# Two-layer H3/MLP training step on one core: where layer 2's normalised rows are kept, and the order of the k-gradient tail

## The chip, the cores and the metric

The kernel runs on one core of a Trainium2 chip. The metric is device time in microseconds for one launch. Before the change three runs gave 770.30, 773.59 and 775.28 us; the median is 773.59. A separate, profiled execution gave the trace that all readings of the kernel before come from.

## The reference

The kernel computes a forward pass and all gradients of it (outputs: the result and the gradients of q, k, v, shift_k, ssm_k, ssm_D, w1, w2). Sequence length S = 2048, width D = 448, hidden width F = 1792, bfloat16.

```
def A(q, k, v, shift_k, ssm_k, ssm_D):       # H3-like long convolution
    k_shift = sum over t of 4: k delayed by t rows * shift_k[:, 3 - t]
    kv = k_shift * v
    y  = irfft(rfft(kv, 2S) * rfft(ssm_k, 2S))[:S] + kv * ssm_D
    return q * y
def B(x, w1, w2):
    return silu(x @ w1) @ w2

x = A_q
for layer in (1, 2):
    x = x + A(layernorm(x), k, v, shift_k, ssm_k, ssm_D)
    x = x + B(layernorm(x), w1, w2)
return x, and vjp(grad_out)
```

The convolution term depends on k, v and the parameters alone, so both layers share it, and its gradient is taken once, from the sum of what both layers give.

## The kernel before

Everything is laid out with 128 partitions; a [2048, 448] matrix stands in on-chip memory as 128 x 16 x 448 (16 row groups, NT = 16). The program has three parts.

`_ssm_prefix` computes the convolution output once by a two-stage Fourier transform in matmuls. `Main.run` walks four chunks of 512 rows through forward and backward of both layers: `H` (x @ w1), `O` (@ w2), `G` (gradient @ w2 transposed, the tile `w2T`), `N` (@ w1 transposed). It leaves the activations and their gradients in device memory as `a_d` and `g_d`, and the normalised rows in `N_d`. `_ssm_suffix` takes the gradient of the convolution: a forward transform (`_fft_stage1`, L206, 16 rounds), transposes (L1095), `spectrum` (L1112), `inverse` (14 chunks of each of two kinds, L226 and L227, a chunk of the kind `cnd` and one of the other by turns), then the gradient with respect to kv (`ps_gkv`, L1169, 8 rounds), that of ssm_k (`ps_gK`, L1189, 8 rounds) with a one-column copy into `gKD` for ssm_D (L1193), that of shift_k (`ps_sk`, L1207, four rounds `r0` of 64, 64, 64 and 32 small matmuls, reduced on VectorE at L1212 to L1215 into `gskb`) and that of k (16 rounds `g` on VectorE, L1223 to L1226, with a store into output 2 after each odd round, L1228). Rounds `g` of 13 and more read three rows that a transfer moves from the next partition (L1177).

The weight gradients of w1 and w2 are done by `Jobs` as filler between the pieces of the third chunk and of the suffix. A job step is four matmuls of 128x448 (L906, or L941 in the opening). There are 224 steps: 24 of an opening, then groups of 8 (two passes of 16 matmuls) or, for the pairs (5, 6) and (12, 13), of 16. Each pass needs one `dstat` tile (512 KB, `load`, L900), loaded on SyncE's queue; the loads are kept in order by `issue_after(self.last_ld.ins)`. The moving operands are whole matrices: `go` (grad_out) and `X` for w2's gradient, `n3m` (layer 2's normalised rows, from `N_d[3]`) and `n1m` (layer 1's) for w1's, and `go2` (grad_out once more) for the rest of w2's. 34 steps run before the suffix; `jobs.run(n)` calls place the others, and `jobs.run(1000)` at the end runs what is left. `n3m` is first read at step 57, `n1m` at 61, `go2` at 169.

Four large places in memory are shared by tag. Before the change WT holds `w2T`, then `Zw` (three of the seven transposed blocks), then `ksf`; WY holds `Ysb` (the prefix's output, then its gradient, read by stage 1), then `n3m`, then `go2`; WB holds `go`, then `n1m`. A tile that follows another waits for the other's last reader. `load_n3` is called after stage 1, when `Ysb` has been read.

The order of TensorE's instructions is that of the program text (`manual_schedule`). For the other engines and the queues a scheduler orders the instructions when the program is built; each engine and queue then runs its list in order. The stores of the suffix are issued by GpSimd (POOL), and so are the loads of spectra and of k, v.

The tile `junk` of the shift gradient and the tile `s_` of the k gradient share one tag, `gka`, with one buffer, and the text puts the reduction of the shift gradient ahead of the 16 rounds.

Of the kernel before, what the change touches and what calls it, by code (L numbers as in the profile page):

```python
# [10 lines left out]
FP32 = mybir.dt.float32  # L11
# [6 lines left out]
P = 128  # L18
# [3 lines left out]
J = 16  # L22
# [816 lines left out]
class Jobs:  # L839
# [78 lines left out]
    def group(self, fts, keys, movs, fin, tags=None):  # L918
        ps = {}
        tags = tags or [None] * len(fts)  # L920
        for i, ft in enumerate(fts):
            st = self.load(keys[0], ft)
            ps[ft] = self.bank(tags[i])
            yield from self.mms(ps[ft], st, movs[0](), 0, NT, True, False)
        if fts == (12, 13):
            self.go2()
        for ft in fts:
            st = self.load(keys[1], ft)
            yield from self.mms(ps[ft], st, movs[1](), 0, NT, False, True)
            fin(ft, ps[ft])  # L930
# [34 lines left out]
    def go2(self):  # L965
        k = self.k
        if not hasattr(self, "go2t"):
            self.go2t = k.wk.tile([P, NT, D], BF16, name="go2", tag="WY")
            k.nc.sync.dma_start(out=self.go2t[:], in_=_pm(k.grad_out[0]))
        return self.go2t  # L970

# [6 lines left out]

    def load_n3(self):
        k = self.k  # L980
        self.n3 = k.wk.tile([P, NT, D], BF16, name="n3m", tag="WY")
        k.nc.sync.dma_start(out=self.n3[:], in_=_pm(k.N_d[3][:]))

    def out(self):
        return self.k.dp2.tile([P, D], BF16, name="dout", tag="dout", bufs=2)
# [64 lines left out]
def _ssm_suffix(k):  # L1050
# [9 lines left out]
    with ExitStack() as es:  # L1060
# [7 lines left out]
        for n2 in range(16):  # L1068
            k.M1sb = k.m1h[n2 // 8]
            _fft_stage1(k, n2, gY[:, n2, :], A1, psum, n2 % 8)  # L1070
            jobs.run(1)
        jobs.load_n3()
        _load_minv(k, nc.gpsimd)
        with ExitStack() as e1:
            p1 = e1.enter_context(tc.tile_pool(name="sspec2", bufs=1, reuse_waits="tile"))
            Zw = k.wk.tile([P, 3, 16, P], BF16, name="Zw", tag="WT")
            Z = [p1.tile([P, 16, P], BF16, name=f"Zg{g}") if g > 2 else Zw[:, g] for g in range(7)]
            Zf = [(z if isinstance(z, bass.AP) else z[:]).rearrange("p a b -> p (a b)") for z in Z]
            kk1 = p1.tile([P, 2, 2048], BF16, name="kk_d", tag="kk1")
            ap = APart(k, e1.enter_context(tc.tile_pool(name="qp", bufs=1, reuse_waits="tile")))  # L1080
            A1f = A1[:].rearrange("p a c n s -> p a (c n s)")

            def spec_load(cp):
                lo, hi = cp * 2048, (cp + 1) * 2048
                kk = (kk0 if cp == 0 else kk1 if cp == 1 else sp.tile([P, 2, 2048], BF16, name="kk_c", tag="kk0") if cp % 2 == 0
                      else p1.tile([P, 2, 2048], BF16, name="kk_d", tag="kk1"))
                nc.gpsimd.dma_start(out=kk[:, 0, :], in_=k.SPEC_d["K"][:, lo:hi])
                nc.gpsimd.dma_start(out=kk[:, 1, :], in_=k.SPEC_d["KV"][:, lo:hi])
                return kk

            kks = [spec_load(0)]
            for g in range(7):
                pt = psum.tile([P, 16, P], BF16, name="ps_tr", **mm)
                for i in range(16):
                    nc.tensor.transpose(pt[:, i, :], A1f[:, 16 * g + i, :], k.ident[:])  # L1095
                if g % 2:
                    nc.scalar.copy(Zf[g], pt[:].rearrange("p a b -> p (a b)"))
                else:
                    i = nc.vector.tensor_copy(Zf[g], pt[:].rearrange("p a b -> p (a b)"))
                jobs.run(1)  # L1100
                if g == 2:
                    ap.run(1, i)
            kks.append(spec_load(1))

            def spectrum(cp):
                xsw = p1.tile([P, 2048], BF16, name="xsw_c", tag="xsw", bufs=2)
                kk = kks[cp]
                for u in range(2):
                    ps = psum.tile([P, 1024], FP32, name="ps_s2", **mm)
                    for hh in range(2):  # L1110
                        c0 = u * 1024 + hh * 512
                        nc.tensor.matmul(ps[:, hh * 512:(hh + 1) * 512], lhsT=k.Gsb[:, G_FWD, :], rhs=Zf[cp][:, c0:c0 + 512], start=True, stop=True)  # L1112
                    nc.scalar.copy(Zf[cp][:, u * 1024:(u + 1) * 1024], ps[:])
                    jobs.run(1)
                _swap_halves(k, xsw, Zf[cp])
                return kk[:, 0, :], kk[:, 1, :], xsw

            def inverse(cp, t):
                for u in range(2):
                    ci = 2 * cp + u  # L1120
                    o = slice(u * 1024, (u + 1) * 1024)
                    for spec_t, B1, cnd in ((t[1], B1k, True), (t[0], B1v_, False)):
                        pa = p1.tile([P, 1024], BF16, name="pa", tag="pab", bufs=5)
                        pb = p1.tile([P, 1024], BF16, name="pb", tag="pab", bufs=5)
                        nc.vector.tensor_tensor(out=pa[:], in0=Zf[cp][:, o], in1=spec_t[:, o], op=ALU.mult)
                        last = nc.vector.tensor_tensor(out=pb[:], in0=t[2][:, o], in1=spec_t[:, o], op=ALU.mult)
                        bal.add("dve", 2.2)
                        _fft_inv_stage2_chunk(k, pa, pb, True, B1, ci, psum, cnd=cnd)
                        jobs.run(3)
                return last  # L1130

            prev = spectrum(0)
            for cp in range(NCI // 2):
                cur = spectrum(cp + 1) if cp + 1 < NCI // 2 else None
                ap.run(1, inverse(cp, prev))
                if cp + 2 < NCI // 2:
                    kks.append(spec_load(cp + 2))
                prev = cur

        p2 = es.enter_context(tc.tile_pool(name="sp2", bufs=1, reuse_waits="tile"))  # L1140
        ksf = k.wk.tile([P, J, D], BF16, name="ksf", tag="WT")
        gks = p2.tile([P, 19, D], BF16, name="gks")
        kx = p2.tile([P, 19, D], BF16, name="kx_s")
        nc.gpsimd.memset(kx[0:1, 0:3, :], 0.0)
# [36 lines left out]
        for dc in range(ND):  # L1181
            gK = p2.tile([DC, S], BF16, name="gK", tag="gK", bufs=3)
            gKv = gK[:].rearrange("p (n1 n2) -> p n1 n2", n2=16)
            for g in range(2):
                py = psum.tile([P, 8, P], FP32, name="ps_gK", **mm)
                for i in range(8):
                    n2 = 8 * g + i
                    for c in range(2):
                        nc.tensor.matmul(py[:DC, i, :], lhsT=B1k[:, 16 * c + n2, dc * DC:(dc + 1) * DC], rhs=k.Minvsb[:, n2, c, :], start=(c == 0), stop=(c == 1))  # L1189
                _copy(nc, nc.scalar, gKv[:, :, 8 * g:8 * g + 8], py[:DC].rearrange("p i n -> p n i"))  # L1190
                jobs.run(2)
            nc.gpsimd.dma_start(out=out5v[:, dc, :], in_=gK[:])
            nc.vector.tensor_copy(gKD[:, dc:dc + 1], gK[:, 0:1])  # L1193
        with nc.allow_non_contiguous_dma(reason="tiny g_D store"):
            nc.gpsimd.dma_start(out=k.outs[6].rearrange("(c p) -> p c", p=DC), in_=gKD[:])

# [5 lines left out]
        for r0 in range(4):  # L1202
            bands = 4 if r0 < 3 else 2
            for sl_ in range(16):
                for b in range(bands):
                    ch = slice(P * r0 + 32 * b, P * r0 + 32 * b + 32)
                    nc.tensor.matmul(pd[32 * b:32 * b + 32, 0, P * r0:P * r0 + P], lhsT=gks[:, sl_, ch], rhs=kx[:, sl_:sl_ + 4, ch], start=(sl_ == 0), stop=(sl_ == 15))  # L1207
        junk = p2.tile([P, 4, 4, 32], FP32, name="skjunk", tag="gka")
        gsk = p2.tile([P, 4, 4], FP32, name="gsk")
        gskb = p2.tile([P, 4, 4], BF16, name="gskb")  # L1210
        for n, lo, hi in ((P, 0, 3), (64, 3, 4)):
            nc.vector.tensor_tensor(out=junk[:n, lo:hi], in0=pd[:n, 0, P * lo:P * hi].rearrange("p (r u c) -> p r u c", u=4, c=32), in1=mask[:n].rearrange("p (a b c) -> p a b c", a=1, b=1).to_broadcast([n, hi - lo, 4, 32]), op=ALU.mult)  # L1212
            nc.vector.tensor_reduce(out=gsk[:n, lo:hi], in_=junk[:n, lo:hi], op=ALU.add, axis=mybir.AxisListType.X)
            for j in range(4):
                nc.vector.tensor_copy(gskb[:n, lo:hi, j], gsk[:n, lo:hi, 3 - j])  # L1215
        jobs.run(4)
        with nc.allow_non_contiguous_dma(reason="tiny g_shift_k store"):
            nc.gpsimd.dma_start(out=k.outs[4][0:384].rearrange("(r p) j -> p r j", p=P), in_=gskb[:, 0:3, :])
            nc.gpsimd.dma_start(out=k.outs[4][384:448], in_=gskb[:64, 3, :])
        s_ = p2.tile([P, 2, D], FP32, name="gka", tag="gka")  # L1220
        for g in range(16):
            pr = R3(4 * (g % 2), 4)
            nc.vector.tensor_tensor(out=pr, in0=gks[:, g:g + 4, :], in1=skb, op=ALU.mult)  # L1223
# [2 lines left out]
            nc.vector.tensor_tensor(out=gk[:, g % 2, :], in0=s_[:, 0, :], in1=s_[:, 1, :], op=ALU.add)  # L1226
            if g % 2:
                nc.gpsimd.dma_start(out=out2_pm[:, g - 1:g + 1, :], in_=gk)  # L1228

        jobs.run(1000)  # L1230

# [29 lines left out]
```

## Time and profile before

| | us |
|---|---|
| median of three runs (lowest, highest) | 773.59 (770.30, 775.28) |
| the profiled execution, its time | 769.31 |
| the profiled execution, its span | 767.5 |
| TensorE busy in the span | 707.8 |
| VectorE busy | 476.4 |
| ScalarE busy | 459.2 |
| GpSimd busy | 127.0 |

The time of the profiled execution is 1.8 us more than its span, and 4.3 us less than the median. In the profile PE is TensorE's matrix multiply, PEld its weight load, DVE is VectorE, ACT ScalarE, POOL GpSimd, SP SyncE's queue of transfers. A row of the timeline gives start and length in us, engine, line, operation, what is written and read, the count, and in brackets how long the engine had been idle and what ended that. A busy share near 100% of TensorE's rows doesn't say that it works at its best rate, since the ends of matmuls are modelled; start to start is read instead.

### The profile page before, as it was taken

Reading aid. Unit: us, or ns where it says so; the run is one execution under the profiler, and the core shown is the slowest. Engines: PE = TensorE matmul, PEld = TensorE weight load, DVE = VectorE, ACT = ScalarE, POOL = GpSimd, SP = SyncE. Lnnn points to the kernel's source line nnn. Section 1 sums busy time; section 2 is a strip of 40 time slices with the busy share of each in tenths; the row PEclk is TensorE's granted clock in tenths of the full one; section 3 lists DMA queues with packets and bytes.
Section 4 is the critical chain, followed back from the end, with each engine's and each line's share of the span. In section 5 each row is a group of like instructions: output and inputs, shape, how many; then the busy total and the mean of one; then the engine's idle time right before and its main releaser. Section 6 shows DMA issues by size and latency. Waiting matters only on the chain.

```text
span 767.5 us, 12748 instructions
## 1 busy us (share of the span) xinstructions
PE 707.8 (92%) x4991; PEld 398.6 (52%) x5020; DVE 476.4 (62%) x1137; ACT 459.2 (60%) x581; POOL 127.0 (17%) x213
## 2 busy tenths in 40 slices
PE   6998779999999999999999999999979999999594
PEld 4976534445444455444445445444646666656352
DVE  4789832857685758855487526444357767760497
ACT  5878767787957878587786772214645454454000
POOL 1144210210020100201001000001212322143211
PEclk9999989999999999999999999999989999999797
DMA  9959769479968996678975993498977897689861
GB/s 319 267 168 292 282 231 233 114 190 226 218 150 187 272 223 169 131 194 210 216 190 115 218 308 131 104 246 251 397 290 243 315 326 243 203 341 364 80 207 60
DMA packets 188653, 171.28 MB, mean 223 GB/s; under 512 B 135954, under 2 KB 166802, under 8 KB 187440
## 3 DMA queue, kind: packets, MB, share of 16 engines
q1 hardware_dynamic: 173984, 113.95, 56.9%
q0 software_dynamic: 14144, 56.50, 22.1%
q8 instruction: 39, 0.64, 0.3%
q14 instruction: 22, 0.18, 0.1%
q10 hardware_dynamic: 464, 0.00, 0.0%
HBM read 73.52 MB, written 60.10 MB: 174 GB/s over the span
## 4 chain that ended last, share of the span: by engine, by line
PE 62%; ACT 12%; DVE 9%; DMA 8%; issue 7%; POOL 2%; SPq 0%; POOLq 0%; ACTq 0%; DVEq 0%
PE ps_d L906 12%; PE ps_h L603 10%; PE ps_n L671 10%; PE ps_g L644 9%; PE ps_o L625 6%; ACT dT L618 3%; DMA n3m<-N_d 2%; PE ps_d L941 2%; DMA M1sb<-c_m 2%; PE ps_v L227 2%; PE ps_v L226 2%; PE ps_t L517 2%; ACT aT L606 1%; DVE ln_st L259 1%; ACT dT L111 1%
## 5 line engine op out<-in xcount | busy, mean ns | idle before, releaser
L906 PEld LDWEIGHTS <-dstat 128*128 128x128 bf16 x800 | 77.0, 99 | 72.4 <-issue 10.4
L603 PE MATMUL ps_h<-nT,w1sb 112*128 112x512 bf16 x448 | 104.4, 379 | 5.5 <-ACT dT L111 2.5
L644 PE MATMUL ps_g<-nT,w2T 128*128 128x512 bf16 x432 | 100.4, 381 | 1.3 <-ACT nT L518 0.2
L671 PE MATMUL ps_n<-w1T,ghT 128*128 128x448 bf16 x448 | 95.3, 353 | 1.8 <-DVE ghT L656 1.7
L625 PE MATMUL ps_o<-w2sb,aT 128*128 128x448 bf16 x448 | 88.8, 352 | 0.0
L654 ACT CAST ghT<-ps_g 128x1024 bf16<-128x1024 f32 (+1 forms) x68 | 54.5, 824 | 49.7 <-PE ps_g L644 49.7
L606 ACT ACTIVATE aT<-ps_h 128x1024 bf16<-128x1024 f32 (+1 forms) x72 | 58.4, 834 | 31.6 <-PE ps_h L603 30.8
L603 PEld LDWEIGHTS <-w1sb 112*128 112x128 bf16 x448 | 43.8, 98 | 58.3 <-issue 8.7
L644 PEld LDWEIGHTS <-w2T 128*128 128x128 bf16 x448 | 43.7, 99 | 50.9 <-issue 1.8
L831 DVE SCALAR_TENSOR_TENSOR lb_v<-lb_u,n 128x448 bf16<-128x448 bf16 x48 | 29.9, 624 | 64.1 <-ACT lb_u L675 63.6
L671 PEld LDWEIGHTS <-ghT 128*128 128x128 bf16 x448 | 43.2, 98 | 44.3 <-DVE ghT L656 4.0
L625 PEld LDWEIGHTS <-aT 128*128 128x128 bf16 x448 | 43.4, 98 | 39.8
L906 PE MATMUL ps_d<-n3m,dstat 128*128 128x448 bf16 x224 | 50.1, 362 | 5.4 <-DMA n3m<-N_d 5.0
L618 ACT ACTIVATE dT<-dT 128x1024 bf16<-128x1024 bf16 (+1 forms) x64 | 54.6, 936 | 0.1
L266 POOL TENSOR_TENSOR rstd<-ln_ve,mhalf 128x2 f32<-128x2 f32 (+2 forms) x27 | 22.6, 836 | 182.4 <-DVE ln_ve L264 182.4
L111 ACT CAST dT<-ps_h 128x1024 bf16<-128x1024 f32 (+1 forms) x59 | 52.1, 901 | 0.0
L906 PE MATMUL ps_d<-n1m,dstat 128*128 128x448 bf16 x224 | 47.8, 352 | 0.1
L226 PE MATMUL ps_v<-Gsb,pa 128*128 128x128 bf16 x336 | 42.9, 219 | 3.1 <-DVE pa L449 3.0
L227 PE MATMUL ps_v<-Gsb,pb 128*128 128x128 bf16 x336 | 42.2, 219 | 2.2 <-DVE pb L450 1.9
L518 ACT COPY nT<-ps_t 128x1024 bf16<-128x1024 bf16 (+1 forms) x28 | 28.3, 1012 | 20.8 <-PE ps_t L517 20.1
L675 ACT ACTIVATE lb_u<-ps_n,rstd 128x448 bf16<-128x448 f32 x32 | 20.7, 646 | 32.2 <-PE ps_n L671 18.1
L906 PE MATMUL ps_d<-X,dstat 128*128 128x448 bf16 x176 | 38.9, 363 | 0.0
(202 smaller groups left out, 1191.7 us busy)
## 6 DMA issues: line engine op xcount, KB each, us to landing
dstat<-g_d SPq DMA_DIRECT2D x28, 512.0 KB, 5.0
dstat<-a_d SPq DMA_DIRECT2D x26, 512.0 KB, 5.6
a_d<-turned SPq DMA_DIRECT2D x16, 512.0 KB, 3.8
g_d<-turned SPq DMA_DIRECT2D x16, 512.0 KB, 3.4
a_d<-turned SPq DMA_DIRECT2D x16, 384.0 KB, 3.1
g_d<-turned SPq DMA_DIRECT2D x16, 384.0 KB, 2.7
N_d<-n POOLq DMA_DIRECT2D x10, 448.0 KB, 5.0
spec_K<-Z POOLq DMA_DIRECT2D x7, 512.0 KB, 7.2
```

The costliest lines, as they stand in the source:

```text
L111: nc.scalar.copy(out, in_)
L226: nc.tensor.matmul(pv[:, i, :], lhsT=pa[:, i * P:(i + 1) * P], rhs=k.Gsb[:, ga, :], start=True, stop=False)
L227: nc.tensor.matmul(pv[:, i, :], lhsT=pb[:, i * P:(i + 1) * P], rhs=k.Gsb[:, gb, :], start=False, stop=True)
L603: nc.tensor.matmul(ps[:, u, :], lhsT=self.w1sb[:, dc, ft * P:(ft + 1) * P], rhs=nT[:DC, dc, :], start=(dc == 0), stop=(dc == ND - 1))
L606: self.last_silu = nc.scalar.activation(aT[hh][:, o:o + hi - lo, :], ps[:, lo:hi, :], ACT.Silu)
L618: self.nc.scalar.activation(d[:, o:o + n, :], d[:, o:o + n, :], ACT.Derivative_silu)
L625: nc.tensor.matmul(po[:, :D], lhsT=aT[ft // 7][:, ft % 7, tl * P:(tl + 1) * P], rhs=self.w2sb[:, ft, :], start=(ft == 0), stop=(ft == NF - 1))
L644: nc.tensor.matmul(ps[:, u, :], lhsT=self.w2T[:, b, ft * P:(ft + 1) * P], rhs=gT[:, b, :], start=(b == 0), stop=(b == ND - 1))
L654: nc.scalar.copy(g, ps[:, lo:hi, :])
L671: nc.tensor.matmul(pn[:, :D], lhsT=gh[ft // 7][:, ft % 7, tl * P:(tl + 1) * P], rhs=self.w1T[:, ft, :], start=(ft == 0), stop=(ft == NF - 1))
L831: nc.vector.scalar_tensor_tensor(out=v[:], in0=u0, scalar=-1.0 / D, in1=n_t, op0=ALU.mult, op1=ALU.mult, accum_out=cp[:, 1:2])
L906: self.nc.tensor.matmul(ps[:, :D], lhsT=st[:, t, :], rhs=mov[:, t, :], start=(first and t == 0), stop=(last and t == NT - 1))
```

## The change

Five edits.

1. `n3m` moves from the tag WY to WT, and `go2` with it; `Zw` and `ksf` move from WT to WY. So `n3m` follows `w2T`, and `Zw` follows `Ysb`.
2. `load_n3` is called inside the group (5, 6), right after the load of that group's first `dstat` tile, and its transfer is tied behind that load on SyncE's queue. The call after stage 1 goes.
3. In `inverse` the chunks that are not `cnd` are followed by two job steps in place of three: 14 steps fewer there.
4. Each of the four rounds `r0` of the shift gradient is followed by three job steps; the four steps after the reduction go. With edit 3, 47 steps are left for the end in place of 41.
5. The reduction of the shift gradient and its two stores move behind round `g` = 11 of the k gradient, with `junk` as a view of `s_`; the copy into `gKD` moves from VectorE to ScalarE.

```diff
         for i, ft in enumerate(fts):
             st = self.load(keys[0], ft)
+            if fts == (5, 6) and i == 0:
+                self.load_n3()
             ps[ft] = self.bank(tags[i])
...
-            self.go2t = k.wk.tile([P, NT, D], BF16, name="go2", tag="WY")
+            self.go2t = k.wk.tile([P, NT, D], BF16, name="go2", tag="WT")
...
-        self.n3 = k.wk.tile([P, NT, D], BF16, name="n3m", tag="WY")
-        k.nc.sync.dma_start(out=self.n3[:], in_=_pm(k.N_d[3][:]))
+        self.n3 = k.wk.tile([P, NT, D], BF16, name="n3m", tag="WT")
+        with k.tc.issue_after(self.last_ld.ins):
+            k.nc.sync.dma_start(out=self.n3[:], in_=_pm(k.N_d[3][:]))
...
-        jobs.load_n3()
         _load_minv(k, nc.gpsimd)
...
-            Zw = k.wk.tile([P, 3, 16, P], BF16, name="Zw", tag="WT")
+            Zw = k.wk.tile([P, 3, 16, P], BF16, name="Zw", tag="WY")
...
                         _fft_inv_stage2_chunk(k, pa, pb, True, B1, ci, psum, cnd=cnd)
-                        jobs.run(3)
+                        jobs.run(3 if cnd else 2)
...
-        ksf = k.wk.tile([P, J, D], BF16, name="ksf", tag="WT")
+        ksf = k.wk.tile([P, J, D], BF16, name="ksf", tag="WY")
...
-            nc.vector.tensor_copy(gKD[:, dc:dc + 1], gK[:, 0:1])
+            nc.scalar.copy(gKD[:, dc:dc + 1], gK[:, 0:1])
...
                     nc.tensor.matmul(pd[32 * b:32 * b + 32, 0, P * r0:P * r0 + P], lhsT=gks[:, sl_, ch], rhs=kx[:, sl_:sl_ + 4, ch], start=(sl_ == 0), stop=(sl_ == 15))
-        junk = p2.tile([P, 4, 4, 32], FP32, name="skjunk", tag="gka")
...
-        jobs.run(4)
...
-        s_ = p2.tile([P, 2, D], FP32, name="gka", tag="gka")
+            jobs.run(3)
+        s_ = p2.tile([P, 2, D], FP32, name="gka")
         for g in range(16):
...
             if g % 2:
                 nc.gpsimd.dma_start(out=out2_pm[:, g - 1:g + 1, :], in_=gk)
+            if g != 11:
+                continue
+            junk = s_[:].rearrange("p a d -> p (a d)")[:, 0:512].rearrange("p (r u c) -> p r u c", u=4, c=32)
...
```

The lines left out at the end are the reduction and the two stores of `gskb`, unchanged.

More of the change, by code (lines that the diff above doesn't have):

```diff
@@ L1207, in _ssm_suffix @@
                     nc.tensor.matmul(pd[32 * b:32 * b + 32, 0, P * r0:P * r0 + P], lhsT=gks[:, sl_, ch], rhs=kx[:, sl_:sl_ + 4, ch], start=(sl_ == 0), stop=(sl_ == 15))
-        junk = p2.tile([P, 4, 4, 32], FP32, name="skjunk", tag="gka")
[L1209 to L1215, printed above, removed]
-        jobs.run(4)
-        with nc.allow_non_contiguous_dma(reason="tiny g_shift_k store"):
-            nc.gpsimd.dma_start(out=k.outs[4][0:384].rearrange("(r p) j -> p r j", p=P), in_=gskb[:, 0:3, :])
-            nc.gpsimd.dma_start(out=k.outs[4][384:448], in_=gskb[:64, 3, :])
-        s_ = p2.tile([P, 2, D], FP32, name="gka", tag="gka")
+            jobs.run(3)
+        s_ = p2.tile([P, 2, D], FP32, name="gka")
         for g in range(16):
@@ L1228, in _ssm_suffix @@
                 nc.gpsimd.dma_start(out=out2_pm[:, g - 1:g + 1, :], in_=gk)
+            if g != 11:
+                continue
+            junk = s_[:].rearrange("p a d -> p (a d)")[:, 0:512].rearrange("p (r u c) -> p r u c", u=4, c=32)
+            gsk = p2.tile([P, 4, 4], FP32, name="gsk")
+            gskb = p2.tile([P, 4, 4], BF16, name="gskb")
+            for n, lo, hi in ((P, 0, 3), (64, 3, 4)):
+                nc.vector.tensor_tensor(out=junk[:n, lo:hi], in0=pd[:n, 0, P * lo:P * hi].rearrange("p (r u c) -> p r u c", u=4, c=32), in1=mask[:n].rearrange("p (a b c) -> p a b c", a=1, b=1).to_broadcast([n, hi - lo, 4, 32]), op=ALU.mult)
+                nc.vector.tensor_reduce(out=gsk[:n, lo:hi], in_=junk[:n, lo:hi], op=ALU.add, axis=mybir.AxisListType.X)
+                for j in range(4):
+                    nc.vector.tensor_copy(gskb[:n, lo:hi, j], gsk[:n, lo:hi, 3 - j])
+            with nc.allow_non_contiguous_dma(reason="tiny g_shift_k store"):
+                nc.gpsimd.dma_start(out=k.outs[4][0:384].rearrange("(r p) j -> p r j", p=P), in_=gskb[:, 0:3, :])
+                nc.gpsimd.dma_start(out=k.outs[4][384:448], in_=gskb[:64, 3, :])
         jobs.run(1000)
```

## The prediction

> **What bounds the kernel now.** I read the page's first rows, then TensorE's waits in the part that the change touches, then the timelines of PE, DVE, POOL and SP around each wait.
>
> ```profile
> span 767.5 us, 12748 instructions
> PE 707.8 (92%) x4991; PEld 398.6 (52%) x5020; DVE 476.4 (62%) x1137; ACT 459.2 (60%) x581; POOL 127.0 (17%) x213
> ...
> q8 instruction: 39, 0.64, 0.3%
> ```
>
> ```profile
> PE ps_sk L1207 <- issue: 7.7, 1, 7.7
> PE ps_d L906 <- DMA n3m<-N_d: 5.0, 1, 5.0
> PE ps_gkv L1169 <- ACT gkv L1171: 1.8, 1, 1.8
> ```
>
> TensorE is busy 92% of the span. These are its three longest waits from 560 us on; two holes, one before `n3m` and one within the shift gradient, are 12.7 us. What a hole costs is more than its length, as the rows after each show:
>
> ```profile
> 563.17 1.65 PE L906 MATMUL ps_d<-n3m,dstat 128*128 128x448 bf16 x4 [5.00 <-DMA n3m<-N_d]
> ...
> 569.35 0.92 PE L906 MATMUL ps_d<-n3m,dstat 128*128 128x448 bf16 x4
> 570.11 0.59 PE L1112 MATMUL ps_s<-Zw,Gsb 128*128 128x512 bf16 x2
> 570.54 0.92 PE L906 MATMUL ps_d<-n1m,dstat 128*128 128x448 bf16 x4
> ...
> 709.06 3.42 PE L1207 MATMUL ps_sk<-kx_s,gks 128*32 128x128 bf16 x212 [0.74 <-DVE gKD L1193]
> 720.18 0.82 PE L1207 MATMUL ps_sk<-kx_s,gks 128*32 128x128 bf16 x12 [7.70 <-issue]
> 720.94 1.67 PE L906 MATMUL ps_d<-go,dstat 128*128 128x448 bf16 x4
> ...
> 726.98 3.19 PE L906 MATMUL ps_d<-go,dstat 128*128 128x448 bf16 x16
> ...
> 754.22 3.19 PE L906 MATMUL ps_d<-X,dstat 128*128 128x448 bf16 x16
> ```
>
> At full pace nine groups of 16 job matmuls take 754.22 - 726.98 = 27.24 us, 3.03 each, so a job step (four) takes 0.76; a pair of L1112 takes 0.43 (570.11 to 570.54). From 563.17 to 569.35 there are three steps and three pairs (four rows between are left out), 3.57 us by these prices, and they took 6.18: the hole at `n3m` costs 5.0 + 2.6 = 7.6. From 720.94 to 726.98 there are 20 job matmuls (the row of 16 is left out), 3.79 us of work in 6.04: the other hole costs 7.7 + 2.2 = 9.9. The granted clock says why:
>
> ```profile
> 560.00:565.00 5.00, 1.83 (x5) 0.69 (x5) 0.03 (x1) 0.00 (x0) 0.55 (x1) 0.67 0.99 390
> ```
>
> The last three columns are clock, DMA share and GB/s: a clock of 0.67, where 1.00 is full speed. [...]
>
> The end is not TensorE's:
>
> ```profile
> 690.30 1.08 DVE L1223 TENSOR_TENSOR B1v<-gks,skx 128x1792 bf16<-128x1792 bf16 x1
> ...
> 721.05 0.75 DVE L1212 TENSOR_TENSOR skjunk<-ps_sk,skmask 128x384 f32<-128x384 f32 x2 [12.00 <-PE ps_sk L1207]
> ...
> 722.90 1.08 DVE L1224 TENSOR_TENSOR gka<-B1v 128x896 f32<-128x896 bf16 x1
> ...
> 724.55 1.08 DVE L1223 TENSOR_TENSOR B1v<-gks,skx 128x1792 bf16<-128x1792 bf16 x1
> ...
> 727.21 1.08 DVE L1223 TENSOR_TENSOR B1v<-gks,skx 128x1792 bf16<-128x1792 bf16 x1
> ...
> 763.07 0.63 DVE L1226 TENSOR_TENSOR B1v<-gka 128x448 bf16<-128x448 f32 x1
> ```
>
> ```profile
> 758.33 0.54 POOL L992 DMA_DIRECT2D out_dram<-dout  x1 [1.73 <-ACT dout L990]
> ...
> 763.99 0.54 POOL L1228 DMA_DIRECT2D out_dram<-B1v  x1 [3.91 <-DVE B1v L1226]
> ```
>
> VectorE starts two of the 16 rounds of the k gradient by 690.30, then its queue holds the reduction of the shift gradient, which TensorE delivers at 721. The rounds run at 727.21 - 724.55 = 2.66 us without a break from 722.90 to 763.70; the span ends 3.5 us after the last store's issue. TensorE's last matmul ends at 757.41 and its store is issued at 758.33; with 3.5 us more that path ends at 761.8.
>
> **The change part by part** (times on the clock of the trace before).
>
> *Reduction behind round 11.* Nothing ahead of the rounds waits for TensorE any more. From 691.4 the rest needs 763.70 - 722.90 = 40.8 us and the reduction 1.85 (721.05 to 722.90): done near 734, some 20 us before TensorE. At round 11, near 721, the wait for `ps_sk` may be short or some us; the margin covers it. The end passes to TensorE: gain 767.5 - 761.8 = **5.7**. The copies into `gKD` cost VectorE 0.16 us each; ScalarE has idle time there, and I cost them at nothing, at most 4 x 0.6 if ScalarE's fixed price is that of its shortest copies.
>
> *`n3m` earlier.* The wait of 5.0 goes, with its 2.6. What is late next is the load behind it on SP's queue, the tile of ft 6:
>
> ```profile
> 529.10 1.62 SPq L900 DMA_DIRECT2D dstat<-a_d  x3
> ```
>
> ```profile
> 535.58 0.55 POOL L199 DMA_DIRECT2D Minvs<-c_minv  x1 [5.79 <-PE ps_d L906]
> ```
>
> ```profile
> q1 hardware_dynamic: 954, 1.92, 89.6%
> ...
> dstat<-a_d SPq DMA_DIRECT2D x3, 512.0 KB, 6.2
> ```
>
> ```profile
> 540.36 0.92 PE L906 MATMUL ps_d<-go,dstat 128*128 128x448 bf16 x4
> ```
>
> Three loads (ft 5, ft 6, ft 5 of the other key) leave SP together at 529.1 to 530.7; `n3m` comes between the first and the second. SP's queue moved 1.92 MB from 528.9 to 535.6, some of it older stores; ft 5, `n3m` and ft 6 are 0.52 + 1.84 + 0.52 = 2.88 MB, so 1.0 to 1.4 MB are left when POOL's loads begin at 535.6. Against these, SP's queue got
>
> ```profile
> q1 hardware_dynamic: 103, 0.36, 47.6%
> ```
>
> ```profile
> q1 hardware_dynamic: 123, 1.66, 78.2%
> ```
>
> in 543 to 545 (180 GB/s, `dstat` tiles) and in 551 to 556 (332 GB/s, `n1m`): ft 6 comes between 538.6 and 543.4, and its first matmul (540.36, the fifth step after the start of ft 5) waits 0 to 3.0. The far bound is from landing times:
>
> ```profile
> n3m<-N_d SPq DMA_DIRECT2D x1, 1792.0 KB, 16.9
> ```
>
> `n3m` took 16.9 us among crowded loads, a `dstat` tile 6.2, so ft 6 could land 10.7 later than now, near 546.8: a wait of 6.4, long enough to lower the clock. I take **1.5**, since `n3m` has the transfers to itself until 535.6. Gain 7.6 - 1.5 = **6.1**. `Zw` now waits for stage 1's last read, which its transposes wait for anyway, and `ksf` for `Zw` as before: nothing.
>
> *Steps between the rounds.* The hole of 7.7 us lies inside a run of independent matmuls. The 39 packets of queue q8 carry 0.64 MB for 4991 + 5020 instructions of PE and PEld: 257 in a packet of 16.4 KB. The burst used 424 in 3.42 us, a packet in 2.1 us, and transfers were slow just then:
>
> ```profile
> DMA packets 111, 0.41 MB, mean 43 GB/s; under 512 B 10, under 2 KB 10, under 8 KB 111
> ```
>
> ```profile
> out_dram<-gKD POOLq DMA_DIRECT2D x1, 0.9 KB, 16.1
> ```
>
> (712.5 to 722.0: 43 GB/s; the 0.9 KB of `gKD` took 16.1 us to land.) I read the hole as code that came late. With three steps behind each round, 64 x 3.42 / 212 = 1.03 us of burst and 2.27 of steps use 152 instructions in 3.30 us, a packet in 5.6 us. If the slow stretch of 9.5 us stays, since the `gKD` store stays, a packet can be late by 0 to 3.9 us; I take 1.5. Gain 9.9 - 1.5 = **8.4**. [...]
>
> *14 steps moved.* TensorE's work is the same, 14 x 0.76 = 10.6 us later. In the inverse loop (window, length, then busy time of PE, PEld, DVE, ACT and POOL)
>
> ```profile
> 640.00:660.00 20.00, 19.95 (x173) 12.84 (x172) 15.37 (x38) 10.09 (x12) 4.64 (x9) 1.00 0.70 224
> ```
>
> TensorE works through and VectorE 15.4 of 20 us, 77%. From the step ahead of the first `ps_v` (570.54) to the last `pb` (665.53, below) are 95 us, with 12 of the 14 steps; at 86 us VectorE's share is 85%. I take **-1.0**, between 0 and the 8.1 left if it does not shrink. Two of the 14 steps do uncover something: those between VectorE's last `pb` and the sixth round of `ps_gkv`.
>
> ```profile
> 665.53 0.69 DVE L1126 TENSOR_TENSOR pb<-xsw_c,kk_c 128x1024 bf16<-128x1024 bf16 x1 [2.09 <-PE ps_v L226]
> ...
> 682.01 1.70 DVE L1174 TENSOR_TENSOR gks<-gkv,gks 128x896 bf16<-128x896 bf16 x3 [2.24 <-DMA gks<-in_A_v_dram]
> ```
>
> The load of `gks`, behind that `pb`, sets when `gkv` buffers come free, and TensorE waits 1.8 for it already: 2 x 0.76 = **-1.5**.
>
> *Queues later.* `go2` waits for `n3m`'s last read, now in the sixth round of `ps_gK`; until its first use TensorE has eight steps, two rounds of `ps_gK` and two of `ps_sk`, some 10 us.
>
> ```profile
> DMA to landing us min/median/max: 8.9/10.8/12.7
> ```
>
> That is the landing of `go` and `go2`: 0 to 2.7 late, **-0.5**. The last `gK` copies wait for stores on POOL's queue, which the 8 stores of output 2 now join:
>
> ```profile
> 707.85 1.01 ACT L111 CAST gK<-ps_gK 112x1024 bf16<-112x1024 f32 x1 [5.02 <-DMA out_dram<-gK]
> ```
>
> **-0.5**, as `go2` no longer loads beside them; the far end is the last rival.
>
> Sum: 5.7 + 6.1 + 8.4 - 1.0 - 1.5 - 0.5 - 0.5 = 16.7. The profiled execution took 769.31 and would take 752.6; the median of the runs shown is 4.3 higher, and 773.59 - 16.7 = **756.9**.
>
> **The rivals.** *The wait moves to ft 6.* The crowded landing of `n3m` speaks for it, the 6 us in which POOL issues nothing against it. 6.4 + 2.6 in place of 1.5: 764.4.
>
> *The inverse loop does not shrink.* VectorE, its loads and ScalarE's copies keep the pace that it has, and the moved steps come on top: 10.6 in place of 2.5, 765.0. None of the waits above shows such a limit; the 85% speaks for a little of it.
>
> *The hole stays*, because it isn't code, or because the slow stretch outlasts any slack; then edit 4 doesn't do its work: 765.3.
>
> *POOL's queue, slower than before.* If n stores of output 2 are queued ahead of the first `gK` store, that store leaves not at
>
> ```profile
> 700.82 0.54 POOL L1192 DMA_DIRECT2D out_dram<-gK  x1 [0.41 <-ACT gK L111]
> ```
>
> but at 689.3 + 5.32 n (two rounds each), and the last `gK` copy and the shift gradient move with it. n = 4 costs 9.8 us, n = 6 20.4; above 16.7, at six, the gain is gone: 777.3. For it: POOL works strictly in order. Against: the `gK` tiles are ready early.
>
> **How the numbers follow.** Forecast 0.60, wait at ft 6 0.11, loop 0.10, hole 0.13, POOL 0.06. About 1% (7.7 us, 765.9) is what a measurement of this kernel can tell from no change. The forecast lies beyond it; the next three lie within 1.5 us of it, and I give a third of the first and half of the two others to "within 1%": 0.15. Slower 0.06, faster 0.79. The forecast's own range is 752 (every unknown cost at nothing: 5.7 + 7.6 + 9.9 - 1.5 = 21.7) to 763 (the costs doubled); with the three near rivals and a microsecond for the measurement it is 750 to 767.
>
> **What would show it.** `n3m` issued near 530 and no wait for it at 558; a wait, if any, at ft 6. No hole in `ps_sk`, or one under 4 us. VectorE's rounds running on from about 15 us earlier than 690, done well ahead of TensorE; a store of `dout` the last but for its landing. From the first `ps_v` to the last `pb` near 86 us. Wrong, if TensorE shows waits for `pa` or `pb` in the loop, or ScalarE waits over 10 us for a `gK` store.

## The result, and the profile after

The changed kernel takes 764.87 us (median of 20 runs, 758.64 to 773.69), the kernel before, run beside it, 773.98 (20 runs, 769.28 to 778.50). The ratio is 0.9874, with 0.9849 to 0.9900 as its 95% interval: 9.1 us faster, where 16.7 were forecast. The profiled execution of the changed kernel took 770.44 us, 5.6 above its median; what made it slow is the best lesson of the case. Runs more than 1.5% above the fastest of their kernel, four of these 20 and the profiled one among them, count in the medians and ranges but not in the ratios.

Its page, first row and row of TensorE (busy us, share of the span, instructions), as they were shown of before:

```profile
span 768.6 us, 12776 instructions
...
PE 712.9 (93%) x5020; PEld 399.1 (52%) x5020; DVE 476.0 (62%) x1133; ACT 460.2 (60%) x585; POOL 126.9 (17%) x213
```

TensorE's waits from 515 to 770 us (total, times, longest):

```profile
PE ps_d L906 <- issue: 12.0, 3, 10.5
PE ps_d L906 <- DMA dstat<-a_d: 3.2, 1, 3.2
...
PE ps_dt L1012 <- issue: 1.6, 1, 1.6
PE ps_gkv L1171 <- ACT gkv L1173: 1.5, 1, 1.5
```

The wait for `n3m` is gone, and a new one of 3.2 stands at a `dstat` tile. No wait stands at the small matmuls `ps_sk` any more, but "issue", time in which nothing visible is waited for, is 13.6 in all in place of 7.9, at job matmuls and one transpose. The timeline of TensorE, with the idle time ahead of a row in brackets:

```profile
546.73 1.67 PE L906 MATMUL ps_d<-go,dstat 128*128 128x448 bf16 x4 [3.17 <-DMA dstat<-a_d]
...
552.56 0.54 PE L206 MATMUL ps_s<-Ysb,M1h 128*128 128x448 bf16 x2
552.94 0.92 PE L906 MATMUL ps_d<-go,dstat 128*128 128x448 bf16 x4
...
572.06 0.92 PE L906 MATMUL ps_d<-n1m,dstat 128*128 128x448 bf16 x4
...
664.92 0.92 PE L1171 MATMUL ps_gkv<-B1v,Minvs 128*128 128x448 bf16 x4
...
678.94 1.06 PE L1191 MATMUL ps_gK<-Minvs,A1g 128*112 128x128 bf16 x16
...
698.73 1.08 PE L1209 MATMUL ps_sk<-kx_s,gks 128*32 128x128 bf16 x64
...
705.12 1.69 PE L906 MATMUL ps_d<-go,dstat 128*128 128x448 bf16 x8 [0.82 <-issue]
...
712.87 0.74 PE L906 MATMUL ps_d<-X,dstat 128*128 128x448 bf16 x3 [0.62 <-issue]
715.16 0.43 PE L1012 MATMUL ps_dt<-ident,dout 128*112 128x128 bf16 x4 [1.56 <-issue]
726.12 5.05 PE L906 MATMUL ps_d<-go,dstat 128*128 128x448 bf16 x16 [10.53 <-issue]
731.02 3.19 PE L906 MATMUL ps_d<-X,dstat 128*128 128x448 bf16 x16
...
761.28 3.19 PE L906 MATMUL ps_d<-X,dstat 128*128 128x448 bf16 x16
```

The first row is the first matmul on ft 6's tile, the load that `n3m` was put ahead of. Three steps and three pairs of stage 1 follow up to 552.94; they took 6.21 where full pace takes 3 x 0.76 + 3 x 0.38 = 3.4 (0.38 from 552.56 to 552.94), so this wait costs 3.2 + 2.8 = 6.0. The big hole now stands ahead of the tail's first group of 16: 13.5 us of issue waits in four pieces, and 731.02 - 726.12 = 4.90 for a group that takes 3.03, so 1.9 more for a lowered clock (0.61 granted from 726 to 731).

The end has passed to TensorE, as the last rows of VectorE and POOL show:

```profile
717.54 0.62 DVE L1217 TENSOR_TENSOR B1v<-gka 128x448 bf16<-128x448 f32 x1 [17.33 <-issue]
...
741.58 0.62 DVE L1217 TENSOR_TENSOR B1v<-gka 128x448 bf16<-128x448 f32 x1
```

```profile
696.48 0.74 POOL L1197 DMA_DIRECT2D out_dram<-gKD  x1 [1.22 <-ACT gKD L1195]
...
765.38 0.54 POOL L995 DMA_DIRECT2D out_dram<-dout  x1 [5.51 <-ACT dout L993]
```

VectorE is done at 742.2 and TensorE at 764.47, so the last store is a `dout`. But VectorE stood still for 17.3 us as well, beside TensorE's hole. The profile calls that "issue" too, but most of it is another wait: the row is that of round 6, which writes the buffer of rounds 0 and 1 again, and the last completion that the trace has of their store to output 2 (issued at 694.12) came at 715.17. So at least 15.0 of the 17.3 us are a store that lands late; in the changed kernel without the store of output 6 the same row waits 5.0 for it. The first row of POOL is the store of output 6 (g of ssm_D: 112 x 4 values of two bytes, 0.9 KB), and 8.5 us behind it the transfers become slow: 16 to 41 GB/s in the four windows of 2 us from 706 to 714. Three rows of the table by stretches follow, the first for the clock behind the wait at ft 6, the others for the transfers; the columns are window, length, busy time (and instructions) of PE, PEld, DVE, ACT and POOL, granted clock, DMA share, GB/s:

```profile
546.00:550.00 4.00, 3.27 (x9) 1.31 (x10) 0.00 (x0) 0.81 (x1) 1.08 (x2) 0.50 1.02 404
...
697.00:705.00 8.00, 7.31 (x162) 4.30 (x158) 3.17 (x4) 3.05 (x5) 2.04 (x4) 1.00 0.99 367
705.00:724.00 19.00, 8.29 (x128) 4.50 (x128) 6.36 (x8) 0.53 (x1) 0.55 (x1) 0.80 1.09 88
```

In 705 to 724 the DMA engines count as busy all the time (1.09) and move 88 GB/s, after 367 just before, and TensorE works 8.3 of 19 us.

### The profile page after: what moved, and what is told of

It reads as the page before. It is cut to its first block, busy times and chain, and to the rows that moved or that the text cites. A ratio compares the mean times of both kernels' runs of the same rounds, so it can differ in the third digit from the quotient of the medians.

```text
span 768.6 us, 12776 instructions
## 1 busy us (share of the span) xinstructions
PE 712.9 (93%) x5020; PEld 399.1 (52%) x5020; DVE 476.0 (62%) x1133; ACT 460.2 (60%) x585; POOL 126.9 (17%) x213
## 4 chain that ended last, share of the span: by engine, by line
PE 65%; ACT 11%; issue 8%; DVE 7%; DMA 5%; POOL 2%; SPq 0%; POOLq 0%; ACTq 0%; DVEq 0%
PE ps_d L906 14%; PE ps_h L603 10%; PE ps_n L671 10%; PE ps_g L644 9%; PE ps_o L625 6%; ACT dT L618 3%; PE ps_d L943 2%; PE ps_v L227 2%; DMA dstat<-a_d 2%; PE ps_v L226 2%; PE ps_t L517 1%; PE ps_s L206 1%; ACT aT L606 1%; DMA K_sb<-in_A_ssm_k_dram 1%; DVE ln_st L259 1%
## 5 line engine op out<-in xcount | busy, mean ns | idle before, releaser
L644 PE MATMUL ps_g<-nT,w2T 128*128 128x512 bf16 x448 | 103.1, 384 | 0.7 <-ACT nT L518 0.7
L906 PE MATMUL ps_d<-go,dstat 128*128 128x448 bf16 x176 | 41.4, 380 | 14.5 <-issue 11.4
L906 PE MATMUL ps_d<-n3m,dstat 128*128 128x448 bf16 x224 | 48.2, 352 | 0.0
```

The source lines that it names most:

```text
L644: nc.tensor.matmul(ps[:, u, :], lhsT=self.w2T[:, b, ft * P:(ft + 1) * P], rhs=gT[:, b, :], start=(b == 0), stop=(b == ND - 1))
L906: self.nc.tensor.matmul(ps[:, :D], lhsT=st[:, t, :], rhs=mov[:, t, :], start=(first and t == 0), stop=(last and t == NT - 1))
```

## The experiments

Each kernel ran beside the kernel before on its chip; times are medians with lowest and highest, ratios are to that kernel with 95% intervals. Two questions: what is the hole in the shift gradient made of (code that comes late by itself, or the slow stretch behind a store), and which of the edits gains or loses.

### The store of output 6

**The changed kernel without it; output 6 is not written.**

```diff
-            nc.gpsimd.dma_start(out=k.outs[6].rearrange("(c p) -> p c", p=DC), in_=gKD[:])
```

> The changed kernel without the store of output 6 (the 448 two-byte elements of gKD; that output is left unwritten). Theory S: this store makes the transfers slow for 10 to 19 us, and TensorE and VectorE then stand still for want of code. Without it the stretch of some 10 to 70 GB/s behind the store is gone, TensorE's waits marked issue between 695 and 730 (13.5 us in all, and 1.9 of lowered clock) fall under 2 us, VectorE's 17.3 us too; time 750 to 757, and the runs spread by 5 us or less in place of 15. Rival W: the stretch comes from the crowd of ordinary stores (gK, output 2, w1's and w2's gradients); then it stays, time 762 to 768, same spread. Rival B: TensorE's bursts of small matmuls cause it; stays too.

756.87 us (752.25 to 759.22), ratio 0.9810 (0.9766 to 0.9855). TensorE's issue waits fall from 13.6 to 0.3, VectorE has none, and the last group starts at 745.84 in place of 761.28. The wait at ft 6's tile, 2.9, is still there.

**The kernel before without it; output 6 is not written.**

> The kernel before without the store of output 6 (left unwritten). Theory S: no slow stretch after 712; the hole of 7.7 us inside the burst shrinks to 0 to 3 us (what is left is code that comes late by itself, since the burst uses a packet of code in 2 us); VectorE's reduction and its 16 rounds start that much earlier and set the end: 773.6 - 5 to 8 = 766 to 769. Rivals W and B: unchanged, 771 to 776.

765.08 us (763.65 to 768.29), ratio 0.9917 (0.9891 to 0.9942). The hole shrinks from 7.7, but something of it stays, at the same place, behind 212 of the small matmuls:

```profile
PE ps_sk L1205 <- issue: 1.4, 1, 1.4
```

TensorE now ends at 749.7, some 10 us ahead of the end that VectorE sets, so most of this gain cannot show.

**The changed kernel with output 6 stored as rows**: TensorE transposes the 112 x 4 values, ScalarE copies them, and the store has four rows of 224 bytes.

```diff
-            nc.gpsimd.dma_start(out=k.outs[6].rearrange("(c p) -> p c", p=DC), in_=gKD[:])
...
+        gDp = k.psum.tile([ND, DC], BF16, name="ps_gD", tag="tr", bufs=1)
+        nc.tensor.transpose(gDp[:], gKD[:], k.ident[:DC, :DC])
+        gDr = p2.tile([ND, DC], BF16, name="gDr")
+        nc.scalar.copy(gDr[:], gDp[:])
+        nc.gpsimd.dma_start(out=k.outs[6].rearrange("(c p) -> c p", p=DC), in_=gDr[:])
```

> The changed kernel with gKD turned by one small transpose on TensorE behind the rounds of the shift gradient, and output 6 stored as four rows of 224 bytes in place of 448 single elements; the output is the reference's. Theory S (single two-byte elements make the stretch slow): same time as without the store, ratio to the kernel before 0.977 to 0.985, no wait marked issue over 2 us behind the shift gradient. Rival W (it matters that anything is stored there): as the changed kernel, 0.985 to 0.99, holes of 5 us and more.

756.57 us (750.97 to 758.16), ratio 0.9786 (0.9738 to 0.9835). The store costs a transpose of 0.21 us and a copy of 0.24, and the row for the window shown above is now

```profile
705.00:724.00 19.00, 18.82 (x188) 10.33 (x188) 18.76 (x32) 1.79 (x4) 5.52 (x9) 1.00 0.77 240
```

TensorE and VectorE work through. The store also moved, from 696.48 to 722.50, so this window shows that the stretch is gone, but not what the new form does. Behind its own issue, from 722.5 to 732.0, the transfers move 238 GB/s, and it landed 6.7 us after its issue, while the next experiment has the old form at 715.11, with a slow stretch behind it. What hurts is the form, not the bytes (0.9 KB in both); which property of the form (the number of pieces, their two bytes or their places) was not tried apart.

**The changed kernel with that store issued twice.**

```diff
             nc.gpsimd.dma_start(out=k.outs[6].rearrange("(c p) -> p c", p=DC), in_=gKD[:])
+            nc.gpsimd.dma_start(out=k.outs[6].rearrange("(c p) -> p c", p=DC), in_=gKD[:])
```

> The changed kernel with the store of output 6 issued twice, one right after the other. Theory S: the slow stretch and the waits marked issue grow by what one store costs, 8 to 19 us: 772 to 785. Rival W: no change within 2 us of the changed kernel (762 to 767).

770.37 us (765.71 to 780.00), ratio 0.9978 (0.9942 to 1.0015): about 8 us more than the changed kernel by the ratios. POOL's rows show what a store of this form takes:

```profile
689.97 0.73 POOL L1197 DMA_DIRECT2D out_dram<-gKD  x1 [2.24 <-ACT gKD L1195]
...
715.11 0.72 POOL L1198 DMA_DIRECT2D out_dram<-gKD  x1 [22.58 <-DMA out_dram<-gKD]
...
734.54 0.55 POOL L1233 DMA_DIRECT2D out_dram<-gskb  x1 [10.17 <-DMA out_dram<-gKD]
```

The second waits for the first, some 25 us after its issue, and a later store waits for the second. There are two slow stretches (48 GB/s from 700 to 705, and 55 to 61 from 720 to 730), and the second, in the tail, costs TensorE waits for `dstat` tiles, 3.9 us in all.

### Code that comes late by itself

**The changed kernel without the store (output 6 is not written) and with edit 4 taken back**: all twelve steps stand behind the four rounds.

```diff
-            jobs.run(3)
+        jobs.run(12)
```

> As the first kernel of this call (no store of output 6), and the twelve steps stand behind the four rounds of the shift gradient, not between them. Theory K: 448 instructions in some 3.5 us outrun the code that comes in packets of 257; a wait marked issue of 1 to 3 us shows inside the burst or right behind it, though no slow stretch is there; 1 to 5 us slower than the first kernel. Rival M: code never comes late by itself; no wait, same time as the first kernel within 1 us.

757.79 us (754.52 to 760.82), ratio 0.9824 (0.9784 to 0.9863): no difference to the kernel without the store that a measurement shows. TensorE's timeline in the shift gradient:

```profile
694.22 2.25 PE L1207 MATMUL ps_sk<-kx_s,gks 128*32 128x128 bf16 x148
700.25 2.12 PE L1207 MATMUL ps_sk<-kx_s,gks 128*32 128x128 bf16 x76 [3.78 <-issue]
```

A burst of small matmuls does stop with no slow transfers near it (401 GB/s from 696 to 701): for 3.8 us here, 1.4 in the kernel before without the store. Where steps stand between the rounds (the changed kernel without the store) the whole rest has 0.3. So edit 4's reason holds, at a few us.

**The changed kernel with edit 4 taken back**, the store as it is; the diff is the last one.

> The changed kernel with edit 4 taken back: the twelve steps stand behind the four rounds of the shift gradient, whose 224 matmuls run in one piece. If edit 4 did what the prediction's step (c) says and shortened the hole, this is slower than the changed kernel by several us: about 770, ratio 0.996. If the hole is the slow stretch behind output 6's store and only falls on other instructions, this is within its noise of the changed kernel: 758 to 766, ratio 0.983 to 0.992, with 4 to 10 us of issue waits at the shift gradient in place of the 10.5 at the tail's first matmuls. If the steps between the rounds are what let the stretch catch TensorE for longer, it is faster: like before with edit 5 alone, 0.983 or less.

764.34 us (756.77 to 772.93), ratio 0.9876 (0.9819 to 0.9933), the changed kernel's own. Issue waits of 7.3 stand in the burst and 0.5 behind it, in place of 13.5 ahead of the tail. With the store left as it is, edit 4 moves the hole and shortens nothing that the time shows.

### The end, and the edits one by one

**The kernel before with edit 5 alone**: the reduction behind round 11, the copy into `gKD` on ScalarE, the four steps straight behind the rounds.

```diff
-        junk = p2.tile([P, 4, 4, 32], FP32, name="skjunk", tag="gka")
...
         jobs.run(4)
...
+            if g != 11:
+                continue
...
-            nc.vector.tensor_copy(gKD[:, dc:dc + 1], gK[:, 0:1])
+            nc.scalar.copy(gKD[:, dc:dc + 1], gK[:, 0:1])
```

> The kernel before with edit 5 alone (reduction behind round 11, copy into gKD on ScalarE; n3m, Zw, ksf, go2 and the steps as before, with the four steps right behind the rounds of the shift gradient). Theory D: the end passes from VectorE to TensorE's last matmul; if the hole in the burst stays near 8 us, 766 to 769. Rival H: with output 2's stores already running, the slow stretch gets longer and the hole grows to 12 to 16 us; then 770 to 775. A hole of 5 us or less: below 764.

759.50 us (756.14 to 768.07), ratio 0.9829 (0.9778 to 0.9880). One edit gives as much as the five together, as far as these intervals tell. Its slow stretch is there as well, and TensorE is hardly touched (columns as above):

```profile
713.50:727.50 14.00, 14.00 (x75) 7.24 (x75) 10.15 (x13) 0.53 (x1) 1.22 (x3) 1.00 0.78 50
```

With 50 GB/s for 14 us TensorE works all the time, on 75 matmuls and 75 weight loads, 150 instructions. In the changed kernel's 19 us it would have worked on 188 and 188, as the row with the store mended shows. By the estimate of 257 to a packet, 376 needed a new one within the stretch, and 150 need none if the last packet came shortly before. The packets of queue q8 agree with that: with the store mended two start between 705 and 724, while in the changed kernel one starts at 702.8 and the next only at 723.8; here one starts at 710.4, just ahead of the stretch, and the next at 719.3. The stretch begins at 713.5, when the shift gradient is over; in the changed kernel it began at 705, between the second and third of its rounds.

**The kernel before with edit 5 and the store as rows**, the two diffs together.

> The kernel before with edit 5 and with output 6 stored as four rows of 224 bytes; edits 1 to 4 left out. If edits 1 to 4 are worth the 7 to 8 us that the prediction gave them beside edit 5, it is that much slower than the changed kernel with the rows: 764, ratio 0.989. If they are worth little once the store is mended, it is within 3 us of that kernel: 756 to 760, ratio 0.979 to 0.985, with a wait for n3m of about 5 and one of 1 to 2 us by issue in the shift gradient still there.

757.33 us (754.35 to 760.25), ratio 0.9818 (0.9771 to 0.9866), with waits of 4.4 for `n3m` and 2.7 by issue in the shift gradient. With all five edits and that store it was 0.9786 (0.9738 to 0.9835): edits 1 to 4 together are worth nothing that these intervals tell from zero, and the store costs edit 5 alone nothing that they show.

**The kernel before with edits 1 and 2 alone**, their diff as in the change.

> The kernel before with edits 1 and 2 alone (n3m in w2T's place, loaded in group (5, 6)). Theory Q: the wait for n3m and its lowered clock (7.6 us) go, and the wait for ft 6's tile takes back 0 to 6 of it, differently from run to run; the end, VectorE's, moves with TensorE: 767 to 773, ratio 0.991 to 0.999. Rival F (the earlier transfer costs more than it saves): above 774.

768.99 us (763.94 to 774.05), ratio 0.9954 (0.9924 to 0.9985). No wait for `n3m` and none at ft 6 in its trace. Its last rows of TensorE and VectorE:

```profile
747.66 3.19 PE L906 MATMUL ps_d<-X,dstat 128*128 128x448 bf16 x16
```

```profile
760.83 0.62 DVE L1228 TENSOR_TENSOR B1v<-gka 128x448 bf16<-128x448 f32 x1
```

TensorE ends at 750.85, and the changed kernel needed 768.6 - 764.47 = 4.1 behind its last matmul: that path would end at 755.0, and the span is 765.3. What TensorE gains, VectorE's end hides.

### Where `n3m` is loaded

**The changed kernel with the load further back**: behind ft 5's second tile, so that ft 6's first tile leaves ahead of it (two loads later on SyncE's queue; the expectations of the two runs after this one count it as one).

```diff
-            if fts == (5, 6) and i == 0:
-                self.load_n3()
...
             st = self.load(keys[1], ft)
+            if fts == (5, 6) and ft == 5:
+                self.load_n3()
```

> The changed kernel with n3m's load two loads later: behind the first tile of the other key, so ahead of one dstat tile in place of three. Theory Q: the wait for ft 6's tile (3.2 us, and 2.8 us of lowered clock after it) comes from n3m's 1.8 MB ahead of it on SP's queue; it goes, nothing takes its place, since n3m still lands before 557: from the start of stage 1 to the first step with n1m 37 us in place of 43.1; time about 6 us under the changed kernel's 764.9, that is 757 to 761. Rival C: transfers are so crowded there that the wait goes to another tile or to n3m: 762 to 767.

762.37 us (757.85 to 766.38), ratio 0.9884 (0.9840 to 0.9929). Neither the wait for `n3m` nor the one at ft 6 is there, but the wait at `ps_gkv` is 5.5 in place of 1.5, and the slow stretch costs 8.5 us of issue waits. No gain that shows.

**The same with the store as rows.**

> The changed kernel with output 6 stored as four rows and n3m's load one transfer later, behind the second set of rows of ft 5. If the wait at ft 6's tile costs the changed kernel 3 to 6 us in its executions and the later load only moves a short wait into the inverse loop, this is the fastest of all: 752 to 754, ratio 0.974 to 0.977. If the wait for n3m's transfer is paid in one place or another (the gkv wait grew from 1.5 to 5.5 us when only the load was moved), it is like the rows alone: 756, ratio 0.979 with 0.974 to 0.984 as its interval.

752.79 us (749.01 to 755.33), ratio 0.9748 (0.9703 to 0.9794). The time is the one expected if the wait at ft 6 costs and nothing takes its place; but something does, the wait at `ps_gkv` is there again:

```profile
PE ps_gkv L1171 <- ACT gkv L1173: 5.7, 1, 5.7
```

**The same with edit 3 taken back**, three steps behind every chunk.

```diff
-                        jobs.run(3 if cnd else 2)
+                        jobs.run(3)
```

> The kernel with output 6 stored as four rows and n3m's load one transfer later, and edit 3 taken back: three steps behind every chunk of the inverse loop. If the shorter loop is only a shift of steps, the time stays: 752 to 757, ratio 0.974 to 0.980, the inverse loop is some 10 us longer and the rest of the job shorter by as much, and the wait at ps_gkv's sixth round, 5.7 us with the shorter loop, falls towards the 1.5 of the kernel before, as the store of q_g has more time. If the shorter loop is worth something by itself (its 14 steps then fill holes behind it), this is slower than 757. If the wait at ps_gkv is a loss that the shorter loop caused, it is faster: 748 to 751, ratio 0.969 to 0.973.

750.35 us (748.37 to 752.14), ratio 0.9740 (0.9700 to 0.9780). TensorE's two longest waits from 515 us on are now

```profile
PE ps_gkv L1171 <- ACT gkv L1173: 2.0, 1, 2.0
PE ps_s L206 <- ACT A1g L111: 1.7, 6, 0.5
```

and this is the fastest kernel of the study, ahead of the changed one by 1.3% of the time before (0.9874 - 0.9740). Against the last kernel, which keeps edit 3, it shows no difference: the wait at `ps_gkv` went, and the time stayed within the intervals.

The lengths of three stretches in the traces, from the starts of the first matmul of stage 1 (L206 in the suffix), of the first on `n1m`, of `ps_gkv` and of `ps_gK` (us):

| kernel | stage 1 to `n1m` | wait there | `n1m` to `ps_gkv` | `ps_gkv` to `ps_gK` |
|---|---|---|---|---|
| before | 44.57 | 5.0, `n3m` | 103.67 | 14.03 |
| before, edit 5 | 44.81 | 5.5, `n3m` | 103.83 | 13.97 |
| before, no store | 43.70 | 5.2, `n3m` | 103.91 | 14.30 |
| before, edit 5, rows | 42.67 | 4.4, `n3m` | 104.01 | 14.19 |
| changed | 43.06 | 3.2, ft 6 | 92.86 | 14.02 |
| changed, no store | 42.90 | 2.9, ft 6 | 94.29 | 13.95 |
| changed, rows | 43.67 | 4.2, ft 6 | 93.88 | 14.07 |
| before, edits 1 and 2 | 39.06 | none | 104.33 | 14.16 |
| changed, store twice | 38.99 | none | 94.23 | 14.21 |
| changed, edit 4 back | 39.68 | 0.4, ft 6 | 94.00 | 18.45 |
| changed, no store, edit 4 back | 39.67 | none | 93.28 | 13.84 |
| changed, load further back | 38.53 | none | 93.52 | 20.01 |
| the same, rows | 37.21 | none | 93.34 | 20.27 |
| the same, edit 3 back | 38.51 | none | 104.32 | 14.24 |

## Why the forecast missed half of the gain

The sum by the profiled executions: the forecast for it was 752.6, it took 770.44, 17.8 more. The prefix, which the change doesn't touch, ran 3.0 later (stage 1 began at 529.00, before at 525.97). `n3m` gave 44.57 - 43.06 = 1.5 in place of 6.1: 4.6 more. The tail holes cost 13.5 + 1.9 where 1.5 was to be left: 13.9 more. The costs of 1.0, 1.5, 0.5 and 0.5 were not paid: 3.5 less. 3.0 + 4.6 + 13.9 - 3.5 = 18.0. The execution lies above its kernel's median, so for the median the misses are smaller: 7.6 in all. The holes are not those of this one execution, though: in the three other traces that have edit 5 and this store after edits 1 and 2 (load further back, store twice, edit 4 back) TensorE's issue waits are 8.5, 10.3 and 7.8. The measured 764.87 lies in the stated range of 750 to 767, but beside the times given for three rivals (764.4, 765.0, 765.3) and not beside 756.9. That the costs of 3.5 were not paid hid a part of the two misses, and that is luck.

**The end passes to TensorE (5.7): right, and the part that pays.** VectorE ends 22 us ahead of TensorE, though it stood still for 17, and edit 5 alone gives 12.2 us by the medians of its chip (771.70 and 759.50). It is worth more than 5.7 where TensorE's own holes are smaller: without the store, or with `n3m` early, VectorE's end lies some 10 us behind TensorE's. The terms of the sum were not independent; the order in which the edits are made decides which of them seems to pay.

**Steps between the rounds (8.4): the term that failed.** The step that failed is "a packet can be late by 0 to 3.9 us; I take 1.5". That a burst stops with no slow stretch near it is shown (3.8 us with no store). But the hole of 7.7 came mostly with the slow stretch: without the store 1.4 of it are left. The forecast let the stretch stay at its place and at 9.5 us; it came in the midst of the rounds, lasted 19, and the tail then waited 10.5 for what the rounds no longer waited for. The rival "the hole stays" was right in its second reason, that the stretch outlasts any slack. That the instructions themselves came late is read from the records of q8's packets. The hole of 10.5 ends 1.3 us after the packet of 723.8 has ended, the first for 20 us, and the `dstat` tile that the matmul behind it reads had landed at 694.7. In eight other traces, four of them without the store or with it as rows, a hole of TensorE ends 1.2 to 1.5 us after such a packet. And in the five traces with neither edit 3 nor edit 4 the hole comes behind the same small matmul, the 212th, whether it lasts 7.7 us (before), 5.0 (edits 1 and 2) or 1.4 to 1.6 (no store; edit 5; edit 5 and rows). Not every hole ends so: those of 7.7 and 5.0 end 7.4 and 4.7 us after their packet, and one of 6.3 with the load further back has no packet near its end. What ended these stays open.

**`n3m` earlier (6.1): mis-sized by the wait at ft 6.** The step "I take 1.5, since `n3m` has the transfers to itself until 535.6" fell: in the changed kernel's trace `n3m` leaves at 533.1 and lands 10.0 us later, and the matmul on ft 6's tile, next in the queue, starts at 546.73. Where the wait comes, it is 2.9 to 4.2 and lowers the clock (a step behind it takes 1.47 in all three, in place of 0.76), which the bounds (0 to 6.4) had and the value taken had not. The table shows that it comes in some executions only, three of the seven with this place for the load (0.4 in a fourth); in the four others the stretch is 4.9 to 5.6 us shorter than the 44.57 of before. With the load further back it is 6.0 to 7.4 shorter in all three, near the 7.6 that the hole at `n3m` was priced at. (The four traces with the old place of the load differ by 2.1 among themselves, 42.67 to 44.81.) What decides between the two was not tried. The row of 546 to 550 shows a clock of 0.50 behind the wait of 3.2, so a wait of this length should have been priced with its clock.

**14 steps moved (-1.0, -1.5): nothing paid at first, but no gain either.** The loop shrank by 103.67 - 92.86 = 10.8, all of the 10.6, and the wait at `ps_gkv` stayed at 1.5. In three of the traces with the shorter loop it is 4.3 to 5.7; where the loop has its steps back, it is 2.0 with the same place of the load. So the term had its reason, and its size was 0 or 4. Why it comes in some traces was not settled. The work moved is the same, and the times with and without edit 3 do not differ.

**`go2` and POOL's queue (-0.5, -0.5): nothing.** No wait for `go2`'s load shows in the changed kernel's trace, and `ps_gkv` to the shift gradient takes 33.81 us (664.92 to 698.73), where it took 34.85 before. That POOL works in order shows where output 6 is stored twice: POOL stands 22.6 us at the second store, and the store of rounds 6 and 7, whose rows VectorE had written by 707.7, leaves behind it at 715.8.

Of the signs given beforehand, those for `n3m`, the loop (85 us from the first `ps_v` to the last `pb`) and the last store came true, and the hole in `ps_sk` did go. VectorE's rounds began at 679.1, some 9 us earlier than before and not 15, and stood still for 17.3, which was not foreseen. The sum failed on a hole that came back behind the rounds.

## What to carry to other kernels

When an engine stops on nothing that the profile shows, look at the transfers, those of code among them: here a store of 0.9 KB made of two-byte pieces had a stretch of 43 to 88 GB/s behind it, and turning it into rows on the chip cost 0.45 us of engine time (0.21 + 0.24). Steps put around a stall don't cure what causes it; they decide only who meets it (ratios 0.9874 with edit 4, 0.9876 with it taken back). And before gains of one engine are summed, see which engine sets the end: until the order of the tail was mended, gains on TensorE could hardly show.

## What the runs showed of the hardware that was not expected

The store of 448 separate two-byte values slowed the transfers for some 10 to 19 us, to 43 GB/s before, 50 with edit 5 alone and 88 after, while the DMA engines still counted as busy (shares of 1.03, 0.78 and 1.09); the same bytes as four rows of 224 did not (238 GB/s in the 9.5 us behind their issue). The slow stretch began 3 us behind the issue before (709.34 to 712.5) and 8.5 behind it after, so where it falls cannot be read from the program.

A run of small matmuls stopped without any of that: in the two traces without the store that have no steps between the rounds, the wait came behind 148 of them in a row (3.8 us) and behind 212 (1.4 us). It ended 1.2 to 1.5 us after a packet of q8, and is read here as code that came late.
